# Eight experts in fixed order and two passes, with all weights kept on chip, after a linear attention

## The chip, the cores and the metric

One core of a Trainium2 chip runs the whole program in one launch. The metric is the device time of one execution in microseconds (us); the median of a few runs counts.

A core has five engines with one instruction queue each, worked in order: TensorE (PE; its weight loads are listed apart as PEld), VectorE (DVE), ScalarE (ACT), GpSimd (POOL) and SyncE (SP). Sixteen DMA engines move data. Loads and stores issued by SP form the hardware queue (q1 in the profile), those issued by POOL the software queue (q0).

## The reference

The input has 4 batches of 8 heads with 768 positions of 64 elements. The first half is a linear attention with decay: per head, `out[i] = sum over j <= i of lam^(i-j) (q_i . k_j) v_j`, worked in blocks with a running 64x64 state. Its result, read as 3072 tokens of 512 elements, is `x`. The second half is a mixture of 8 experts with balanced routing:

```python
logits = x @ w_gate                       # 3072 x 8
order = np.argsort(-logits.flatten())     # all token-expert pairs, best first
for idx in order:
    tok, e = idx // 8, idx % 8
    if assigned[tok] >= 0 or counts[e] >= 384: continue
    assigned[tok] = e; counts[e] += 1
for e in range(8):
    h = np.maximum(x[assigned == e] @ w1[e], 0)   # 512 -> 1024
    out[assigned == e] = h @ w2[e]                # 1024 -> 512
```

Each expert gets exactly 384 tokens. The greedy order can be run in steps: up to the moment when a first expert is full, every token simply goes to its best expert (the filling step); then the tokens that are left choose among the others until the next is full, and so on. On the inputs used here the filling step ends with 356, 363, 375, 340, 384, 317, 327 and 350 tokens at the eight experts, and 260 tokens are left.

## The kernel before

**Attention** (`_Attn.run`, L903). 24 tiles of 128 tokens. An iteration loads q, k and v of tile s+3 by SP (L747 to L751), turns and multiplies, writes the finished tile s-1 to `x_dram` by SP (L876) and prepares k and v of tile s+2 (`prep`, L754). The buffers of the loads hold four tiles, and SP works its queue in order, so a load stands behind the write of an earlier tile. The eight logits of each token are left in the tile `logits` (L901).

**Routing** (`_Router`). `phase1` runs once all logits are there: the range of the values (L102 to L124), three rounds that narrow down the rank at which the first expert is full (`count`, L148: a comparison on DVE, 24 matmuls, a sum, a maximum), the slots, and the list `perm` of the first full expert's tokens (L227 to L230). A second set of 24 matmuls (L272) gathers the tokens that are left and the token table `tok1`. `phase(i)` then finds the next full expert, again in three rounds (L327 to L343), and its `perm`.

**Experts** (`_Moe`). Which expert comes next is known only from the routing, so its number is read into a register by POOL (L469), and POOL issues its two weight loads of 1 MB each as stored on chip (L475, L477; float32 in memory, cast to bf16 on the way; three buffers each), three gathers of 128 token rows (L461), and, as the expert's results come, three scatters of 128 rows to the output (L503). `ffn` (L480) turns the rows (L486), multiplies by `w1` (L492, 32 matmuls of 384 columns), and by `w2` (L499, 24 of 512 columns). A scatter waits until the scatter before it has landed, since both write the same tensor at rows unknown beforehand.

`_check_and_mend` (L526) runs a slow exact path if a flag says that the fast routing does not hold.

What sets the order: a scheduler places the instructions of each engine's queue by their dependences and its own estimate of time; the order of the Python lines is only its starting point. For the expert stretch of the new kernel PE, POOL and DVE are taken out of that and follow the order of the code.

Of the kernel before, what the change touches and what calls it, by code (L numbers as in the profile page):

```python
# [13 lines left out]
I32 = mybir.dt.int32  # L14
AX = mybir.AxisListType
# [7 lines left out]
class _Router:  # L23


    def __init__(self, ctx, tc, identf, identb):
        nc = tc.nc
        self.nc, self.tc = nc, tc
        self.identf, self.identb = identf, identb
        P = 128  # L30
        self.rc = ctx.enter_context(tc.tile_pool(name="rconst", bufs=1))

    def constants(self):
        nc, rc, P = self.nc, self.rc, 128
        i_kt = rc.tile([P, P, 24], BF16, name="i_kt")
        nc.gpsimd.iota(i_kt, pattern=[[1, P], [0, 24]], base=0, channel_multiplier=0,
                       allow_small_or_imprecise_dtypes=True)
        self.i_kt = i_kt
        i_j = rc.tile([P, 29, 24], BF16, name="i_j")
        nc.gpsimd.iota(i_j[:, 0:5], pattern=[[1, 5], [0, 24]], base=24, channel_multiplier=0,  # L40
                       allow_small_or_imprecise_dtypes=True)
        nc.gpsimd.iota(i_j[:, 5:29], pattern=[[1, 24], [0, 24]], base=0, channel_multiplier=0,
                       allow_small_or_imprecise_dtypes=True)
        self.i_j = i_j
        i_t = rc.tile([P, 29, 24], BF16, name="i_t")
        nc.gpsimd.iota(i_t, pattern=[[0, 29], [128, 24]], base=0, channel_multiplier=0,
                       allow_small_or_imprecise_dtypes=True)
        self.i_t = i_t
        i_p = rc.tile([P, 1], F32, name="i_p")
        nc.gpsimd.iota(i_p, pattern=[[0, 1]], base=0, channel_multiplier=1,  # L50
                       allow_small_or_imprecise_dtypes=True)
        self.i_p = i_p
        i_e = rc.tile([P, 8], F32, name="i_e")
        nc.gpsimd.iota(i_e, pattern=[[1, 8]], base=0, channel_multiplier=0,
                       allow_small_or_imprecise_dtypes=True)
        self.i_e = i_e
        kio = []
        for r, sc in enumerate((65536, 256, 1)):
            i_k = rc.tile([P, P], BF16, name=f"i_k{sc}")
            nc.vector.tensor_scalar(i_k, i_kt[:, :, 0], float(sc), None, OP.mult)  # L60
            kio.append(i_k)
        self.kio = kio
# [928 lines left out]
```

## Time and profile before

| | |
|---|---|
| runs | 393.26 us median of 3 (392.68 to 394.55) |
| profiled execution | 392.43 us, its span 390.7 us |
| attention, to the last logits | 0 to 163.4 us |
| routing to the first row list | 163.4 to 188.5 us |
| first turn of the first expert | 199.2 us |
| last matmul of the last expert | about 371 us |
| last scatter issued | 384.4 us |
| PE busy | 262.1 us (67%), mean granted clock 0.847 |
| DMA | 52.00 MB written, q0 36.5% and q1 30.0% of 16 engines |

How to read it: the span runs from the first to the last instruction of the profiled execution. A busy share is a mean over stages with different limits: in the attention DVE, PE and ACT are all near 75% busy, and in the expert stretch PE stands still for ten microseconds at a time while the DMA engines are full. The granted clock is the share of full speed at which TensorE ran; it takes two levels, 2.4 GHz (1.0) and 1.2 GHz (0.5).

### The profile page before, as it was taken

How to read it: one execution, taken by the hardware profiler on the slowest of the kernel's cores; microseconds unless marked ns; L12 is line 12 of the kernel's file. 1: busy time of each engine (PE TensorE's matmuls, PEld its weight loads, DVE VectorE, ACT ScalarE, POOL GpSimd, SP SyncE). 2: the span in 40 equal slices, each digit the busy share in tenths (PEclk: the TensorE clock that was granted, in tenths of full speed). 3: DMA queues.
4: the chain of work that ended last, by engine and by line, in shares of the span. 5: the costliest groups of instructions: out<-in, count | busy, mean ns of one | idle time of the engine just before them, and what ended most of it. 6: DMA issues, size and time to landing. Idle time of an engine off the chain costs nothing. (4 is left out here: it accounts for less than half of the span.)

```text
span 390.7 us, 8518 instructions
## 1 busy us (share of the span) xinstructions
PE 262.1 (67%) x3323; PEld 179.6 (46%) x3331; DVE 196.1 (50%) x701; ACT 170.2 (44%) x308; POOL 160.9 (41%) x180
## 2 busy tenths in 40 slices
PE   2787787878787778542679459850774939796900
PEld 2567666766666676342334234520433525443400
DVE  3977677676866777668347630700523516400000
ACT  4686776767675766300024124520332414443400
POOL 5857565566566655201301415152351422514122
PEclk9999999999999999755559758995695886997975
DMA  8988878687776821100940997549396793999321
GB/s 154 217 188 173 194 161 181 154 181 172 156 177 149 202 63 37 56 0 4 180 74 6 190 222 95 109 95 196 100 167 142 137 174 79 156 209 142 93 81 55
DMA packets 96973, 52.00 MB, mean 133 GB/s; under 512 B 76960, under 2 KB 88224, under 8 KB 96928
## 3 DMA queue, kind: packets, MB, share of 16 engines
q0 software_dynamic: 17920, 26.22, 36.5%
q1 hardware_dynamic: 79008, 25.19, 30.0%
q8 instruction: 27, 0.44, 0.5%
q14 instruction: 18, 0.15, 0.1%
HBM read 58.74 MB, written 12.58 MB: 183 GB/s over the span
## 5 line engine op out<-in xcount | busy, mean ns | idle before, releaser
L492 PE MATMUL p<-xeT,w1t 128*128 128x384 bf16 x256 | 60.2, 382 | 4.9 <-ACT xeT L487 4.9
L503 POOL DMA_INDIRECT out_dram<-oe,perm x24 | 24.2, 1008 | 88.7 <-ACT hT L495 30.3
L812 POOL TENSOR_SCALAR_AFFINE_SELECT sp<-sp 128x512 f32<-128x512 f32 x48 | 34.9, 735 | 41.4 <-DVE sp L809 41.4
L487 ACT COPY xeT<-pt 128x512 bf16<-128x512 bf16 x24 | 14.1, 586 | 82.3 <-PE pt L486 68.0
L495 ACT ACTIVATE hT<-p 128x384 bf16<-128x384 f32 x64 | 31.4, 491 | 33.7 <-PE p L492 29.0
L499 PE MATMUL p<-w2t,hT 128*128 128x512 bf16 x184 | 42.9, 379 | 1.3 <-DMA w2t<-in_moe_w_dram 0.9
L809 DVE TENSOR_TENSOR sp<-S,sp 128x512 bf16<-128x512 f32 x48 | 33.0, 736 | 21.4 <-ACT sp L808 20.4
L486 PE MATMUL pt<-identb,xe 128*128 128x128 bf16 x96 | 12.9, 271 | 41.9 <-DMA xe<-x_dram,perm 35.0
L808 ACT CAST sp<-S 128x512 bf16<-128x512 f32 x48 | 32.1, 740 | 16.9 <-PE S L803 16.9
L492 PEld LDWEIGHTS <-w1t 128*128 128x128 bf16 x256 | 26.7, 112 | 22.5 <-issue 15.5
L766 POOL TENSOR_TENSOR vl<-vs,vh 128x512 bf16<-128x512 f32 x24 | 27.8, 1160 | 16.4 <-ACT vh L764 16.0
L461 POOL DMA_INDIRECT xe<-x_dram,perm x24 | 24.6, 1024 | 23.6 <-PE p L492 9.3
L761 POOL TENSOR_TENSOR vs<-vf,lamneg 128x512 f32<-128x512 f32 x24 | 27.8, 1159 | 3.8 <-ACT lamneg L731 3.8
L803 PE MATMUL S<-qh,kT 64*128 64x128 f16 x384 | 28.7, 221 | 0.9 <-DVE sp L809 0.5
L486 PEld LDWEIGHTS <-xe 128*128 128x128 bf16 x96 | 8.5, 117 | 45.0 <-DMA xe<-x_dram,perm 37.7
L499 PEld LDWEIGHTS <-hT 128*128 128x128 bf16 x192 | 18.5, 97 | 22.1 <-issue 1.1
L502 ACT COPY oe<-p 128x512 f32<-128x512 f32 x24 | 14.1, 586 | 33.1 <-PE p L499 26.4
L843 PE MATMUL XL<-vh,sp 128*128 128x64 bf16 x384 | 23.2, 194 | 7.3 <-POOL sp L812 6.9
L775 PE MATMUL kT_ps<-identf,kp 128*128 128x128 f32 x96 | 16.1, 291 | 14.1 <-DVE kp L759 14.1
L843 PEld LDWEIGHTS <-sp 128*128 128x128 bf16 x576 | 20.2, 98 | 11.0 <-POOL sp L812 10.4
L475 POOL DMA_DIRECT2D w1t<-in_moe_w_dram x8 | 6.7, 836 | 44.3 <-DVE Z L407 24.1
L764 ACT CAST vh<-vs 128x512 bf16<-128x512 f32 x24 | 14.9, 621 | 19.0 <-POOL vs L761 19.0
(244 smaller groups left out, 630.4 us busy)
## 6 DMA issues: line engine op xcount, KB each, us to landing
w1t<-in_moe_w_dram POOLq DMA_DIRECT2D x8, 1024.0 KB
w2t<-in_moe_w_dram POOLq DMA_DIRECT2D x8, 1024.0 KB, 12.0
qf<-in_q_dram SPq DMA_DIRECT2D x24, 256.0 KB, 3.5
kf<-in_k_dram SPq DMA_DIRECT2D x24, 256.0 KB, 4.3
vf<-in_v_dram SPq DMA_DIRECT2D x24, 256.0 KB, 5.0
x_dram<-xs SPq DMA_DIRECT2D x24, 256.0 KB, 2.2
xe<-x_dram,perm POOLq DMA_INDIRECT x24, 9.5
out_dram<-oe,perm POOLq DMA_INDIRECT x24, 9.1
```

The source lines that it names most:

```text
L461: nc.gpsimd.indirect_dma_start(out=xe[:, c, :], out_offset=None, in_=self.x_dram, in_offset=bass.IndirectOffsetOnAxis(ap=perm[:, c : c + 1 ...
L492: nc.tensor.matmul(p1, w1t[:, kc, fc * P : (fc + 1) * P], xeT[:, kc].rearrange("p c s -> p (c s)"), start=(kc == 0), stop=(kc == 3))
L495: nc.scalar.activation(hT[:, fc, :], p1, ACT.Relu)
L499: nc.tensor.matmul(p2, hT[:, kc, c * P : (c + 1) * P], w2t[:, kc, :], start=(kc == 0), stop=(kc == 7))
L503: nc.gpsimd.indirect_dma_start(out=self.out, out_offset=bass.IndirectOffsetOnAxis(ap=perm[:, c : c + 1], axis=0), in_=oe, in_offset=None, ...
L761: nc.gpsimd.tensor_tensor(vs, vf, self.lamneg[:, t, :, None].to_broadcast([P, 8, 64]), OP.mult)
L766: nc.gpsimd.tensor_tensor(vl, vs, vh, OP.subtract)
L803: nc.tensor.matmul(S[a][:, hp, :], kT[r, hp, :, ks], qq[r, hp, :], start=(i == 0), stop=(i == 2))
L808: nc.scalar.copy(s[:, :, :, 1], S[a])
L809: nc.vector.tensor_tensor(s[:, :, :, 0], S[a], s[:, :, :, 1], OP.subtract)
L812: nc.gpsimd.affine_select(out=sf, in_=sf, compare_op=OP.is_ge, fill=0.0, base=0, pattern=[[0, 4], [1, P]], channel_multiplier=-1)
L843: nc.tensor.matmul(X[a][:, hp, :], sp[a][:, hp, :, ss], vv[:, h, :], start=(first and hp == 0 and i == 0), stop=(i == 2), skip_group_check ...
```

## The change

Three things are rewritten together.

Routing: the range of the values is taken from the first 18 tiles while the attention still runs, and the rank of each tile's tokens is prepared beside it (`ranges`, `ranks`, called by the hook). The three counting rounds use 128, 64 and 64 thresholds, the last two with half-size comparisons. After the filling step each expert's first 256 tokens are known. The remaining six steps (`steps`) run piece by piece between the experts' matmuls; the code waits in between by an estimate (`WAIT`).

Experts: they come in the order 0 to 7. Pass one takes 256 rows of each (two row blocks), pass two the last 128. All sixteen weight tiles have their own place on chip. Nine loads are written in the attention's code (`load_w(0)` to `load_w(8)`), seven between the experts.

Where the moves land is read from the instruction order. First POOL in the early attention. `vs` and `vl` prepare v of a tile, `sp` is its masked score tile, `w_0_78` and `w_0_79` are w1 and w2 of expert 0. Before:

```order
L812 AFFINE_SELECT sp_225<-sp_225 128x512
L766 TENSOR_TENSOR vl<-vs,vh 128x512
L812 AFFINE_SELECT sp_229<-sp_229 128x512
L761 TENSOR_TENSOR vs<-vf,lamneg 128x512
L766 TENSOR_TENSOR vl<-vs,vh 128x512
L812 AFFINE_SELECT sp_333<-sp_333 128x512
```

And POOL at the same place now:

```order
L979 AFFINE_SELECT sp_238<-sp_238 128x512
L979 AFFINE_SELECT sp_242<-sp_242 128x512
L73 AFFINE_SELECT slt<-slt 128x128
L533 DMA w_0_78<-in_moe_w_dram 128x4x1024
L928 TENSOR_TENSOR vs<-vf,lamneg 128x512
L535 DMA w_0_79<-in_moe_w_dram 128x8x512
L933 TENSOR_TENSOR vl<-vs,vh 128x512
L979 AFFINE_SELECT sp_346<-sp_346 128x512
```

The scheduler has moved the first loads from the end of the attention, where the code writes them, to its second tile; all nine stand between the selects of tile 0 and those of tile 7.

Second, POOL when pass one begins. `perm` lists rows, `xe` are gathered rows, `oe` a finished block; DMASW is a slot of the software queue, of which there are eight. Before, at the first experts:

```order
L461 DMA xe<-x_dram,perm 128x512 [waits DMASW1_49]
L503 DMA out_dram<-oe,perm 3072x512 [waits DMASW2_49,Activation_49]
L469 TENSOR_LOAD ei [waits DVE_49]
L469 ISA x2
L475 ISA
L475 DMA w1t<-in_moe_w_dram 128x4x1024 [waits DMASW3_49]
```

And now:

```order
L550 DMA xe<-x_dram,perm_4180 128x512 [waits DMASW0_49]
L550 DMA xe<-x_dram,perm_4180 128x512 [waits DMASW1_49]
L533 DMA w_5_3839<-in_moe_w_dram 128x4x1024 [waits DMAHW3_49,DMAHW2_49,DMASW2_49]
L535 DMA w_5_3840<-in_moe_w_dram 128x8x512 [waits DMASW3_49]
L600 DMA out_dram<-oe,perm_4055 3072x512 [waits DMASW4_49,Activation_49]
L600 DMA out_dram<-oe,perm_4055 3072x512 [waits DMASW5_49,DMASW4_49,Activation_49]
L550 DMA xe<-x_dram,perm_4180 128x512 [waits DMASW6_49,PE_49]
L550 DMA xe<-x_dram,perm_4180 128x512 [waits DMASW7_49]
L533 DMA w_6_3841<-in_moe_w_dram 128x4x1024 [waits DMASW0_49]
L535 DMA w_6_3842<-in_moe_w_dram 128x8x512 [waits DMASW1_49]
L600 DMA out_dram<-oe,perm_4055 3072x512 [waits DMASW5_49,DMASW2_49,Activation_49]
```

Loads no longer wait for a register, but the pairs of experts 5, 6 and 7 each stand right ahead of the first scatter of experts 0, 1 and 2; the second scatter waits for the slot of the first.

Third, PE where the first expert starts. L486 and L564 are the first turns. Before, they come right behind the matmuls of the left-over tokens:

```order
L272 LDWEIGHTS A
L272 MATMUL psC<-R,A 128x207
L486 LDWEIGHTS xe
L486 MATMUL pt<-identb,xe 128x128
L486 LDWEIGHTS xe
```

Now two counting rounds and the token table (`psT`, 24 matmuls, L339) come in between; the last rows ahead of the turns are:

```order
L388 LDWEIGHTS ind
L388 MATMUL cps<-oh,ind 128x8
L404 LDWEIGHTS ones_572
L404 MATMUL nps<-S,ones_572 128x8
L564 LDWEIGHTS xe
L564 MATMUL pt<-identb,xe 128x128
```

So the first expert's turns stand behind the second round of the first later step. The diff, cut to its core:

```diff
+    def ranks(self, L, a, b):
...
+        V.tensor_tensor(self.ind1[:, :, a:b], q1[:, None, :].to_broadcast([P, P, n]),
+                        self.i_kt[:, :, a:b], OP.is_ge)
...
+            for hh in range(2):
...
+                V.tensor_tensor(ind[:, 0:64, ts], zq[:, None, ts].to_broadcast([P, 64, 12]),
+                                self.i_kt[:, 0:64, ts], OP.is_ge)
...
+        yield perm0.rearrange("p (e j) -> p e j", j=3)
...
+        psC = ps.tile([P, 18, 5], F32, tag="pos")
...
+            psT = ps.tile([P, 2, 24], F32, tag="pos")
...
+    def steps(self, rest):
...
+        for i in range(1, 7):
...
+            for r in range(3):
+                ind = sp.tile([P, 5, P], BF16, tag="indc")
+                for c in range(5):
+                    V.tensor_scalar(ind[:, c, :], self.kvec[r], zr[:, c : c + 1], None, OP.is_le)
...
+                yield self.WAIT[0 if r else (1 if i > 1 else 2)]
...
+                yield self.WAIT[3]
...
+                if i == 1 and r == 0:
+                    yield rest()
...
+    def load_w(self, m):
+        e = m // 2
+        if m % 2 == 0:
+            self.nc.gpsimd.dma_start(out=self.w1t[e], in_=self.w1r[e])
+        else:
+            self.nc.gpsimd.dma_start(out=self.w2t[e], in_=self.w2r[e])
...
+    def gather(self, perms):
+        nc, P = self.nc, 128
+        xe = self.mp.tile([P, 2, 512], BF16, tag="xe", bufs=4)
...
+                for kc in range(4):
+                    nc.tensor.matmul(p1[:, f, 0:n, :], self.w1t[e][:, kc, fc * P : (fc + 1) * P],
+                                     j["xeT"][:, kc, 0:n, :], start=(kc == 0), stop=(kc == 3),
+                                     skip_group_check=True)
...
+        oe = self.mp.tile([P, 512], F32, tag="oe", bufs=4)
+        nc.scalar.copy(oe, p2)
+        nc.gpsimd.indirect_dma_start(
+            out=self.out, out_offset=bass.IndirectOffsetOnAxis(ap=j["perms"][c], axis=0),
+            in_=oe, in_offset=None, bounds_check=3071, oob_is_err=False)
...
+    with tc.manual_schedule(engines={E.PE, E.Pool, E.DVE}):
...
+            for n in range(16):
+                if n == 0:
+                    yield ("land", 6.0)
+                    yield from moe.turn(jobs[0])
+                if n == 8:
+                    yield ("routed", None)
+                    yield from moe.turn(jobs[8])
+                yield from moe.up(jobs[n], n % 8)
+                if n < 15 and n != 7:
+                    yield from moe.turn(jobs[n + 1])
+                if jobs[min(n + 3, 15)] is None:
+                    ahead(n + 3)
+                for _ in range(2):
+                    if later:
+                        moe.load_w(later.pop(0))
+                for c in range(len(jobs[n]["perms"])):
+                    yield from moe.down(jobs[n], n % 8, c)
...
+        def hook(s):
+            if s == 2:
+                router.constants()
+            if 19 <= s <= 21:
+                router.ranges(logits, 18, attn.pt, "T", s - 19)
+            if s == 22:
+                router.ranks(logits, 0, 10)
+            if s == 23:
+                router.ranks(logits, 10, 20)
+            if s == 24:
+                router.ranks(logits, 20, 23)
+            if 21 <= s <= 24:
+                moe.load_w(s - 21)
...
+    for m in range(4, 9):
+        moe.load_w(m)
+    fi = _route_and_moe(ctx, tc, logits, router, moe, range(9, 16))
```

## Rows read from the trace of the kernel before

**Rows 1.** Waits, summed: who, for whom, us, times, longest
```profile
ACT xeT L487 <- PE pt L486: 68.0, 22, 34.8
```
**Rows 2.** Tile `xe`: from issue to landing
```profile
DMA to landing us min/median/max: 8.8/9.5/11.2
```
**Rows 3.** Timeline of POOL: start, us, what, [idle before]
```profile
238.40 0.97 POOL L477 DMA_DIRECT2D w2t<-in_moe_w_dram  x1
239.67 1.05 POOL L503 DMA_INDIRECT out_dram<-oe,perm  x1 [0.30 <-issue]
250.14 1.00 POOL L503 DMA_INDIRECT out_dram<-oe,perm  x1 [9.41 <-ACT hT L495]
```
**Rows 4.** Timeline of POOL, the last scatter
```profile
384.45 0.98 POOL L503 DMA_INDIRECT out_dram<-oe,perm  x1 [2.51 <-issue]
```
**Rows 5.** Windows: length, busy of PE, PEld, DVE, ACT, POOL, clock, DMA share, GB/s
```profile
60.00:80.00 20.00, 15.88 (x336) 13.68 (x337) 15.50 (x26) 14.47 (x26) 11.85 (x13) 1.00 0.77 171
203.00:371.00 168.00, 117.95 (x732) 63.39 (x740) 55.32 (x406) 57.13 (x109) 53.56 (x55) 0.81 0.74 135
```
**Rows 6.** Windows with one DMA queue full: attention's loads, then weights
```profile
8.00:10.00 2.00, 1.76 (x8) 1.43 (x8) 0.66 (x3) 1.99 (x5) 0.93 (x1) 1.00 1.34 218
187.00:188.00 1.00, 1.00 (x17) 1.00 (x17) 0.23 (x1) 0.00 (x0) 0.00 (x0) 0.50 1.10 209
```
**Rows 7.** The page's DMA issues, and timelines of SP and ACT
```profile
kf<-in_k_dram SPq DMA_DIRECT2D x24, 256.0 KB, 4.3
...
64.56 0.65 SPq L749 DMA_DIRECT2D kf<-in_k_dram  x1
...
71.74 0.78 ACT L758 CAST kp<-kf 128x512 f16<-128x512 f32 x1
...
77.79 0.79 ACT L758 CAST kp<-kf 128x512 f16<-128x512 f32 x1
```
**Rows 8.** Timeline of DVE, routing: last logits, counting rounds two and three, row list
```profile
163.27 0.17 DVE L901 COPY logits<-Lo 128x8 f32<-128x8 f32 x1 [0.52 <-PE Lo L899]
...
172.29 1.83 DVE L153 TENSOR_TENSOR ind<-z,i_kt 128x1536 bf16<-128x1536 bf16 x2
...
176.10 1.83 DVE L153 TENSOR_TENSOR ind<-z,i_kt 128x1536 bf16<-128x1536 bf16 x2
...
188.33 0.17 DVE L230 TENSOR_REDUCE perm<-pe 128x3 int32<-128x6 f32 x1 [1.10 <-PE pe L227]
```
**Rows 9.** Timeline, routing matmuls, the first turn and the first finished block
```profile
186.54 1.75 PE L227 MATMUL pe<-B1v,A 128*128 128x6 bf16 x24 [4.41 <-DVE B1v L222]
...
194.48 4.93 PE L272 MATMUL psC<-R,A 128*128 128x207 bf16 x13
...
199.22 0.60 PE L486 MATMUL pt<-identb,xe 128*128 128x128 bf16 x4
...
212.97 0.59 ACT L502 COPY oe<-p 128x512 f32<-128x512 f32 x1 [1.53 <-PE p L499]
```
**Rows 10.** Timeline of DVE, one counting round of a later step to the next
```profile
206.77 0.91 DVE L331 TENSOR_SCALAR ind<-i_k,zn 128x128 bf16<-128x128 bf16 x5
...
208.84 0.91 DVE L331 TENSOR_SCALAR ind<-i_k,zn 128x128 bf16<-128x128 bf16 x5
```
**Rows 11.** Timeline of PE, matmuls back to back
```profile
203.06 1.44 PE L492 MATMUL p<-xeT,w1t 128*128 128x384 bf16 x4 [0.67 <-ACT xeT L487]
...
206.09 0.97 PE L492 MATMUL p<-xeT,w1t 128*128 128x384 bf16 x5
...
207.12 0.32 PE L492 MATMUL p<-xeT,w1t 128*128 128x384 bf16 x1
...
215.24 1.89 PE L499 MATMUL p<-w2t,hT 128*128 128x512 bf16 x8
```
**Rows 12.** The page's DMA queues: packets, MB, share of 16 engines
```profile
q0 software_dynamic: 17920, 26.22, 36.5%
q1 hardware_dynamic: 79008, 25.19, 30.0%
```

More of the change, by code (lines that the diff above doesn't have):

```diff
@@ L167, in phase1 @@
+        cps = ps.tile([P, 8], F32, tag="cnt")
+        for t in range(23):
+            nc.tensor.matmul(cps, self.ind1[:, :, t], ohb[:, t, :], start=(t == 0), stop=False)
+        self.ranks(L, 23, 24)
+        nc.tensor.matmul(cps, self.ind23, ohb[:, 23, :], start=False, stop=True)
+        _, nm1 = settle(cps, self.ones[64])
+        self.more(23, 24)
         z2 = sp.tile([P, 24], BF16, name="z2")
-        nc.vector.tensor_scalar(z2, z12, nm1, 200.0, OP.subtract, OP.min)
+        V.tensor_scalar(z2, self.q2, nm1, 100.0, OP.subtract, OP.min)
@@ new lines, in down @@
+    def down(self, j, e, c):
+        nc, P = self.nc, 128
+        p2 = self.mps.tile([P, 512], F32, tag="p2")
+        for kc in range(8):
+            nc.tensor.matmul(p2, j["hT"][:, kc // 2, kc % 2, c, :], self.w2t[e][:, kc, :],
+                             start=(kc == 0), stop=(kc == 7))
+            if kc % 2 and kc < 7:
+                yield 0.43
+        oe = self.mp.tile([P, 512], F32, tag="oe", bufs=4)
[3 more added lines that the diff above has]
+            in_=oe, in_offset=None, bounds_check=3071, oob_is_err=False)
+        yield 0.43
@@ new lines, in ffn, with _route_and_moe, ahead, experts @@
+    def ffn(self, e, perms):
+        j = self.gather(perms)
+        for g in [self.turn(j), self.up(j, e)] + [self.down(j, e, c) for c in range(len(perms))]:
+            for _ in g:
+                pass
+def _route_and_moe(ctx, tc, L, router, moe, later):
+    E = mybir.EngineType
+    with tc.manual_schedule(engines={E.PE, E.Pool, E.DVE}):
+        gen = router.phase1(ctx, L)
+        jobs = [None] * 16
+        perm0 = next(gen)
+        for e in range(2):
+            jobs[e] = moe.gather([perm0[:, e, 0:1], perm0[:, e, 1:2]])
+        later = list(later)
+        perm1 = perm2 = None
+        def ahead(n):
+            if perm1 is None or n > 15:
+                return
+            if n < 8:
+                jobs[n] = moe.gather([perm1[:, n, 0:1], perm1[:, n, 1:2]])
+            elif perm2 is not None:
+                jobs[n] = moe.gather([perm2[:, n - 8 : n - 7]])
+        def experts():
+            for n in range(16):
[15 more added lines that the diff above has]
+                    yield from moe.down(jobs[n], n % 8, c)
+        ex = experts()
+        t, done, want = 0.0, False, None
+        r_at = None
+        def route():
+            nonlocal r_at, perm1, perm2, t
+            while True:
+                got = next(gen, None)
+                if got is None:
+                    r_at = None
+                    return
+                if isinstance(got, float):
+                    r_at = t + got
+                    return
+                if perm1 is None:
+                    perm1 = got
+                    ahead(2)
+                    moe.load_w(later.pop(0))
+                else:
+                    perm2 = got
+                    for n in (8, 9, 10):
+                        ahead(n)
+        route()
+        while not done or r_at is not None:
+            if r_at is not None and (r_at <= t or done or
+                                     (want is not None and (want[0] == "routed" or r_at <= want[1]))):
+                t = max(t, r_at) + 0.2
+                route()
+                continue
+            if want is not None:
+                t = t + 5.0 if want[0] == "routed" else max(t, want[1])
+                want = None
+            got = next(ex, None)
+            if got is None:
+                done = True
+            elif isinstance(got, tuple):
+                want = got
+            else:
+                t += got
```

776 lines of the change are left out of this document (396 added, 380 removed).

## The prediction

> **What bounds the kernel now.** I read the slices of the span first, then the windows, the summed waits, and POOL's timeline. The program has three stretches. In the attention (to 163.4 us) the engines share the work: DVE, PE and ACT are each near 75% busy, and the DMA engines move 171 GB/s [rows 5]. Routing is a chain on DVE and PE. The expert stretch, 203 to 371 us, is bound by no engine: PE is busy for 118 of 168 us, POOL and DVE for a third [rows 5]. What ends last there is a gather: turning the rows waits 68 us in sum [rows 1], because a gather lands 9.5 us after its issue [rows 2], behind the two weight loads that the same step has just put into the same queue. The last scatters then stand alone, one per 3.5 us, since each waits for the landing of the one before (2.51 idle + 0.98 busy), and 6.2 us pass from the start of the last to the end of the span, so 2.7 us beyond its own 3.5 [rows 4].
>
> **Attention with nine weight loads in it.** The change takes the loads off the expert stretch; it pays for that here. A weight tile is 1.05 MB as stored, and the software queue alone writes 209 GB/s, so one load fills the DMA engines for 5.1 us, nine for 45.6. A tile of the attention moves four times 0.262 MB; its loads alone saturate at 218 GB/s [rows 6], which makes 4.8 us, while the tile takes 6.06 us of compute (77.79 - 71.74) [rows 7]. The nine loads stand in POOL's queue between the selects of tile 0 and tile 7, about 6.5 tiles apart. In that stretch the DMA engines have 45.6 + 6.5 x 4.8 = 76.8 us of work against 6.5 x 6.06 = 39.4 us of compute: 37 us too much. Loads run ahead: the k issued at 64.56 lands some 4.3 us after it and is read at 77.79, three ACT reads later by the order of the code, so 8 us are in hand [rows 7]. That leaves 29 us by which the attention ends later; afterwards compute at 6.06 us a tile sets the pace again and nothing is caught up. No trace of before shows both queues full at once, so this has ends: 0, if the two queues use different limits of an engine and the loads hide altogether (a gain is excluded: traffic is only added), and 45.6, if none of it hides. I take 29, the sum from the saturated rows. POOL's own issue of the nine, 0.97 each [rows 3], stands beside a POOL that is 59% busy here [rows 5]; without that cover it would be 9 us.
>
> DVE gets the ranges and ranks, some 60 small instructions (about 12 us) in the last six tiles, where it has 4.5 us free in 20 [rows 5], 8 us in six tiles, and more once no tile is prepared any more. I take +2; ends 0 and 12.
>
> **From the last logits to the first expert.** Before, 163.44 to 188.5 us [rows 8]. Five microseconds of range finding go to the attention; what is left of them for the last tile is about six DVE operations, 1.2 us. Rounds two and three, 3.81 us each (176.10 - 172.29), lose half of their 1.83 us of comparison and keep the rest: 2.9. The row list for experts 0 and 1 is ready at about 163.4 + 1.2 + 1.5 + 2 x 2.9 + 8.2 = 180 us, 8 earlier, and its gathers find the queue empty. But PE's order does not let the first turns follow. In between stand: 2 us of DVE for the left-over table; 24 matmuls of 90 columns (between 0.073 us at 6 columns and 0.38 at 207 [rows 9], so 0.2 each, 4.8); 2.2 us to the first thresholds; a round, 1.6; the token table on DVE, 1.6; 24 matmuls of 48 columns, 3.4; ten small DVE operations and the second round, 3.6. That sums to 19 us and ends at 199, where the first turn stood before (199.22) [rows 9]. So the shorter routing is given away to what was put ahead of the first turn; the weights being there gains nothing yet.
>
> **The expert stretch.** PE's work: at full clock a row of five matmuls of 384 columns takes 0.97 and a single one 0.32, so 0.16 each, and eight of 512 in 1.89 are 0.22 each [rows 11]. Pass one has 256 up matmuls of 256 columns (0.107: 27), pass two 256 of 128 (0.055: 14), both together 192 down matmuls (42), turns and routing pieces about 15 (estimate from the same spacings). That is 98 us, from 199 to 297 if nothing stops it, plus a few us at the lower clock at the start.
>
> The scatters are a longer chain. There are still 24, each waits for the one before. The first is ready about 12 us after the first turn (before: 212.97 - 199.22 = 13.75 with three row blocks instead of two [rows 9]): at 211. Alone a scatter costs 3.5 us [rows 4]; behind a weight load it costs 10.5 (239.67 to 250.14, with a load issued just ahead) [rows 3]. By POOL's new order the pairs of experts 5, 6 and 7 each stand straight ahead of a scatter, that of experts 0, 1 and 2. So 21 x 3.5 + 3 x 10.5 = 105 us. Two gathers of 1.3 us fit nearly into the 2.5 us between scatters; the three issued at once after the last routing step and the weight issues do not: +4. End: 211 + 105 + 4 + 2.7 = 322.7. PE runs beside it and is held back where four finished blocks wait, so its 98 us do not count again.
>
> The routing beside it: a round takes 2.07 us [rows 10], a step with its tail about 8, six steps and the end 55 us, from 190 to some 250; pass two begins near 280. It is hidden; if each step stopped PE for its whole excess over the code's estimate, about 1.2 us, it would be 7 us on a PE that has 20 to spare.
>
> **Sum.** 322.7 + 29 + 2 = 353.7 us of span; 1.7 us lie around the span (392.43 - 390.7), so 355.4 for an execution like the profiled one, whose time is 0.8 below the median of the runs: 356 us.
>
> **Rivals.** *The loads hide in the attention.* For it: the share of the DMA engines reads 1.34 when the loads saturate but only 0.77 in the steady attention [rows 5, 6], so much of their time may be free for another queue. Against: in bytes, 171 of 218 GB/s are in use. With 0 to 10 us instead of 29: about 332.
>
> *The loads of q, k and v starve.* If the two queues take turns packet by packet, the weights' packets are the long ones: 36.5% of 390.7 us on 16 engines over 17920 packets is 127 ns, 30.0% over 79008 is 24 ns [rows 12]. Then the attention's loads get 24/151 = 16% of the time while weights flow; the nine take 45.6/0.84 = 54 us, in which loads for 1.8 tiles come, with the 8 us in hand worth 19 us of compute: 35 us late, up to 45.6 if the prefetch cannot refill between pairs. About 368. No run of before shows it, since nothing but the weights' own queue is active when they load. The Trainium skill, DMA: Bandwidth & Descriptors, section Queues, rings and completion order, says that each DMA engine goes round its queue rows packet by packet, and that is the rule which speaks against putting large loads beside many small ones; no row here shows it.
>
> *TensorE stays at its lower clock: slower than before.* Over the expert stretch the granted clock was 0.81 [rows 5], the rest of full speed lost after the waits for gathers; at the lower level four up matmuls take 1.44 us instead of five in 0.97 [rows 11]. If the many small routing matmuls and stops of pass one hold the clock at 0.5, the 98 us of PE become 196: 199 + 31 + 196 + 7 for the last scatter = 433. It decides from the point where PE's end passes the scatters' gain: at full clock PE's path ends at 335, before ends at 391, so from 56 us more, a little over half of the stretch at the lower level. Against: in 203 to 217 us before, with counting rounds between expert matmuls, the spacing fell to that of the full clock at 206 [rows 11].
>
> *The change does not do what it says.* If an expert had fewer than 256 tokens at the filling step, the slow exact path would run after the fast one. The inputs give 317 to 384, so it is left out but for 1%.
>
> **Chances.** Forecast 0.50 (own range 343 to 364), hidden 0.24 (325 to 343), starved 0.17 (364 to 378), lower clock 0.07, the rest 0.02. A measurement here can tell about 0.5% (2 us) from no change. Faster 0.92, same 0.01, slower 0.07. The range leaves out the lower clock and the outer end of the hidden case, and so runs from 327 to 386.
>
> **What would show it.** In the profile after: nine weight loads issued before some 90 us and tiles of more than 6.1 us there, DMA share near its maximum; the last logits near 194 instead of 163.4; the row list 17 us after them, the first turn 36 us after them; three scatters of 10 us early in pass one, then a beat of 3.5 us to the end; PE's clock at 1.0 for most of the stretch. I am wrong in the attention if its tiles keep 6.1 us (hidden) or if q, k and v land 20 us after issue (starved); wrong in the expert stretch if POOL is not waiting for its own scatters when PE stands still.

## The result, and the profile after

| | before | after |
|---|---|---|
| median of the runs | 393.08 us (392.68 to 394.55) | 374.79 us (374.2 to 375.93) |
| ratio | | 0.9532, interval 0.9498 to 0.9566 |
| span of the profiled execution | 390.7 us | 373.2 us |
| last logits | 163.4 us | 197.8 us |
| first turn of the first expert | 199.2 us | 230.6 us |
| first scatter, last scatter | | 242.5 us, 365.3 us |
| PE busy | 262.1 us (67%) | 268.0 us (72%) |

The kernel became 18.3 us faster. I had forecast 356 us, 37 us less than before. The direction and the order of events came as predicted; the expert stretch was 17 us longer and the attention 3 us longer than the sum. Executions of one kernel differ by up to 3.5%, so the times below are medians, while places in time come from one profiled execution each.

The attention first. Here are the windows of the kernel after, with the columns of [rows 5]:

```profile
40.00:60.00 20.00, 6.46 (x110) 5.44 (x108) 4.39 (x9) 4.19 (x8) 5.07 (x6) 0.67 1.18 219
...
80.00:100.00 20.00, 13.35 (x183) 11.41 (x184) 9.40 (x16) 10.15 (x18) 7.61 (x9) 0.61 1.08 218
```

From 40 to 60 us the engines do 30 to 41% of their work of before, PE 6.46 of 20 us where before it had 15.88 [rows 5], while the DMA engines move 219 GB/s, as much as when one queue alone saturates them [rows 6]. Who waits stands in the summed waits of the kernel after (us, times, longest):

```profile
ACT kp L925 <- DMA kf<-in_k_dram: 27.6, 7, 11.1
...
ACT oe L599 <- DMA out_dram<-oe,perm: 22.8, 4, 10.8
```

Before, ACT waited for k once, for 3.0 us; now it loses 27.6 us in seven waits. DVE's timeline shows the end of the attention and the row list, against 163.27 and 188.33 in [rows 8]:

```profile
197.60 0.22 DVE L1068 COPY logits<-Lo 128x8 f32<-128x8 f32 x1
...
214.46 0.17 DVE L289 TENSOR_REDUCE perm<-pe 128x6 int32<-128x12 f32 x1 [1.11 <-PE pe L286]
```

PE's timeline of the kernel after shows what stands between the row list and the first turn (before: [rows 9]):

```profile
216.37 4.11 PE L303 MATMUL psC<-R,ind 128*128 128x90 f16 x24 [1.95 <-DVE R L300]
...
225.15 2.36 PE L339 MATMUL psT<-R,ind 128*128 128x48 f16 x24 [1.73 <-DVE R L336]
...
230.61 1.01 PE L564 MATMUL pt<-identb,xe 128*128 128x128 bf16 x8
```

Then POOL's timeline, with scatters (L600), gathers (L550) and weight loads (L533, L535); it answers to [rows 3, 4]:

```profile
242.53 1.07 POOL L600 DMA_INDIRECT out_dram<-oe,perm  x1 [6.60 <-ACT oe L599]
252.99 1.03 POOL L600 DMA_INDIRECT out_dram<-oe,perm  x1 [9.40 <-ACT oe L599]
...
256.72 0.83 POOL L533 DMA_DIRECT2D w<-in_moe_w_dram  x1
257.52 0.98 POOL L535 DMA_DIRECT2D w<-in_moe_w_dram  x1
258.80 1.06 POOL L600 DMA_INDIRECT out_dram<-oe,perm  x1 [0.30 <-issue]
273.26 1.03 POOL L600 DMA_INDIRECT out_dram<-oe,perm  x1 [13.40 <-ACT oe L599]
...
277.77 0.98 POOL L535 DMA_DIRECT2D w<-in_moe_w_dram  x1
279.06 1.06 POOL L600 DMA_INDIRECT out_dram<-oe,perm  x1 [0.30 <-issue]
294.30 1.03 POOL L600 DMA_INDIRECT out_dram<-oe,perm  x1 [14.19 <-ACT oe L599]
...
365.31 0.98 POOL L600 DMA_INDIRECT out_dram<-oe,perm  x1 [3.75 <-ACTq L696]
```

The three scatters behind the weight pairs hold the next one back for 10.46, 14.46 and 15.24 us. (The pair of the first was issued from 234.18 us on, 8 us ahead of its scatter; the other two stand right ahead of theirs, behind two gathers.) The releaser named is ACT's copy into a block buffer, but that copy itself waits for a landed scatter (the second row of the waits above), so both names point at the same landing. From 268 to 308 us PE does 24 us of work in 40, as these windows of the kernel after show:

```profile
268.00:288.00 20.00, 14.33 (x110) 9.70 (x109) 8.04 (x49) 4.37 (x7) 5.94 (x6) 0.83 0.77 138
288.00:308.00 20.00, 9.99 (x70) 6.46 (x67) 5.57 (x36) 5.56 (x10) 8.24 (x8) 0.74 0.51 107
```

### The profile page after: what moved, and what is told of

It reads as the page before. It is cut to its first block, busy times and chain, and to the rows that moved or that the text cites. A ratio compares the mean times of both kernels' runs of the same rounds, so it can differ in the third digit from the quotient of the medians.

```text
span 373.2 us, 8812 instructions
## 1 busy us (share of the span) xinstructions
PE 268.0 (72%) x3551; PEld 210.7 (56%) x3551; DVE 185.6 (50%) x587; ACT 168.2 (45%) x297; POOL 161.6 (43%) x189
## 5 line engine op out<-in xcount | busy, mean ns | idle before, releaser
L581 PE MATMUL p<-xeT,w 128*128 128x256 bf16 (+1 forms) x512 | 53.9, 262 | 17.7 <-ACT hT L586 16.4
L600 POOL DMA_INDIRECT out_dram<-oe,perm x24 | 24.3, 1014 | 81.0 <-ACT oe L599 49.6
L581 PEld LDWEIGHTS <-w 128*128 128x128 bf16 x512 | 42.0, 103 | 27.6 <-issue 19.3
L594 PE MATMUL p<-w,hT 128*128 128x512 bf16 x192 | 47.5, 392 | 0.0
L586 ACT ACTIVATE hT<-p 128x512 bf16<-128x512 f32 (+1 forms) x64 | 31.1, 491 | 22.4 <-PE p L581 16.6
L976 DVE TENSOR_TENSOR sp<-S,sp 128x512 bf16<-128x512 f32 x48 | 32.9, 734 | 15.4 <-ACT sp L975 15.2
L1010 PE MATMUL XL<-vh,sp 128*128 128x64 bf16 x384 | 27.7, 208 | 12.8 <-POOL sp L979 12.5
L550 POOL DMA_INDIRECT xe<-x_dram,perm x24 | 25.2, 1050 | 25.2 <-DVE B L294 11.2
L568 ACT COPY xeT<-pt 128x1024 bf16<-128x1024 bf16 (+1 forms) x16 | 12.8, 798 | 42.9 <-PE pt L564 42.7
L925 ACT CAST kp<-kf 128x512 f16<-128x512 f32 x24 | 18.9, 789 | 27.6 <-DMA kf<-in_k_dram 27.6
L926 DVE TENSOR_TENSOR kp<-kf,kp 128x512 f16<-128x512 f32 x24 | 19.6, 816 | 23.4 <-ACT kp L925 23.4
L942 PE MATMUL kT_ps<-identf,kp 128*128 128x128 f32 x96 | 19.3, 338 | 15.8 <-DVE kp L926 11.0
L970 PEld LDWEIGHTS <-kT 64*128 64x128 f16 x576 | 20.9, 104 | 10.3 <-issue 6.9
L1029 PE MATMUL stp<-vh,kp 128*128 128x128 bf16 x160 | 22.0, 252 | 4.7 <-ACT vh L931 3.9
```

Source lines behind the costliest of these rows:

```text
L550: nc.gpsimd.indirect_dma_start(out=xe[:, c, :], out_offset=None, in_=self.x_dram, in_offset=bass.IndirectOffsetOnAxis(ap=pm, axis=0), boun ...
L581: nc.tensor.matmul(p1[:, f, 0:n, :], self.w1t[e][:, kc, fc * P : (fc + 1) * P], j["xeT"][:, kc, 0:n, :], start=(kc == 0), stop=(kc == 3), ...
L586: nc.scalar.activation(hT[:, fp, :, 0:n, :], p1[:, :, 0:n, :], ACT.Relu)
L594: nc.tensor.matmul(p2, j["hT"][:, kc // 2, kc % 2, c, :], self.w2t[e][:, kc, :], start=(kc == 0), stop=(kc == 7))
L600: nc.gpsimd.indirect_dma_start(out=self.out, out_offset=bass.IndirectOffsetOnAxis(ap=j["perms"][c], axis=0), in_=oe, in_offset=None, bound ...
L970: nc.tensor.matmul(S[a][:, hp, :], kT[r, hp, :, ks], qq[r, hp, :], start=(i == 0), stop=(i == 2))
```

## The experiments

Two theories were to be tested. **A:** the attention's 34 us are DMA time of nine loads beside q, k and v. **B:** the chain of scatters, with the weight pairs in its queue, sets the length of the expert stretch. The rivals: the routing work beside the attention, TensorE's own pace, the later routing steps. Where a load is to start late, VectorE first writes one column of its tile from a logits tile, so that the scheduler cannot place the load earlier (`pin`).

**1. Nine loads at the attention's end.** The diff, with the pin:

```diff
+    def load_w(self, m, after=None):
...
+        if after is not None:
+            w = (self.w2t if m % 2 else self.w1t)[e]
+            self.nc.vector.tensor_copy(w[:, 0, 0:1], after)
...
-                moe.load_w(s - 21)
+                moe.load_w(s - 21, logits[:, s - 2, 0:1])
...
-        moe.load_w(m)
+        moe.load_w(m, logits[:, 23, 0:1])
```

> Nine weight loads tied to the last tiles of the attention (two fall in the last two tiles, seven behind the last select), nothing else changed. Theory A (attention): the 34 us by which the last logits came later are DMA time of the nine loads beside q, k and v. Then the last logits return to 164 to 167 us, the first turn follows 33 to 36 us later (200), and the span is 373 - 32 = 341 (338 to 346). Rival: the routing work that now runs beside the attention (ranges, ranks on VectorE) or the new order costs a good part of it; then the last logits stay at 175 or later and the span above 350.

Measured: 354.12 us (351.85 to 358.97), ratio 0.8981 [0.8944, 0.9017]. The profiled execution took 358.97 us. Its last logits came at 175.97, just in the rival's range: 21.6 us of the 34 are gone, 12.7 are not. In the expert stretch the long periods stayed, and the first turn waited 4.5 us for a gather that stood behind seven loads. So early loads are the larger part of the 34 us, and something else is in it: the logits of tile 19 come at 155.3, before at 145.7, and no load is issued until then (the first at 155.99).

**2. The other seven loads ahead of the experts.** Attention as in the changed kernel; loads 9 to 12 behind it, the first of them pinned to the last logits, 13 to 15 behind the first gathers:

```diff
+        while later:
+            moe.load_w(later.pop(0))
...
-    for m in range(4, 9):
-        moe.load_w(m)
+    for m in range(4, 13):
+        moe.load_w(m, logits[:, 23, 0:1] if m == 9 else None)
...
```

> Attention as in the changed kernel; the last seven loads are issued right behind the attention and behind the first gathers, none ahead of a scatter. Theory B (the chain of scatters paces the experts, and weight pairs ahead of a scatter cost 10 to 15 us each): the three long periods (10.5, 14.5, 15.2 us) become 4 us each, so the span falls by about 27 us, to 346 (340 to 352), and POOL still waits for its own scatters to the end. Rival (TensorE's work with the routing pieces paces them, the scatters only follow): at most 8 us are won, span 365 or more.

Measured: 340.72 us (340.36 to 345.0), 0.8664 [0.8639, 0.8689], at the lower end of the forecast. The first scatter starts where it did (241.98 against 242.53). POOL's timeline of this run, scatters L603, gathers L553:

```profile
241.98 1.05 POOL L603 DMA_INDIRECT out_dram<-oe,perm  x1 [8.43 <-ACT oe L602]
245.56 1.00 POOL L603 DMA_INDIRECT out_dram<-oe,perm  x1 [2.53 <-ACT hT L589]
246.87 1.04 POOL L553 DMA_INDIRECT xe<-x_dram,perm  x1 [0.30 <-PE p L584]
248.21 1.02 POOL L553 DMA_INDIRECT xe<-x_dram,perm  x1 [0.30 <-issue]
250.63 1.03 POOL L603 DMA_INDIRECT out_dram<-oe,perm  x1 [1.40 <-ACT oe L602]
254.21 1.00 POOL L603 DMA_INDIRECT out_dram<-oe,perm  x1 [2.54 <-ACT hT L589]
...
335.07 0.98 POOL L603 DMA_INDIRECT out_dram<-oe,perm  x1 [3.38 <-ACTq L700]
```

No period is long any more, and the 23 periods take 93.1 us (335.07 - 241.98) instead of 122.8 (365.31 - 242.53). The loads in the chain's way cost 29.7 us, B's price. The window of this run from the first turn to the last product shows what sets the pace without them, a PE that is busy nearly throughout:

```profile
230.84:333.20 102.36, 99.28 (x924) 69.91 (x936) 41.18 (x246) 55.86 (x104) 41.74 (x42) 0.97 0.45 103
```

**3. Loads spread over the attention, the rest ahead of the experts.** One load each at tiles 0, 4, 8, 12 and 16, four at the last tiles, the seven as in 2:

```diff
+            if s in (2, 6, 10, 14, 18):
+                moe.load_w((s - 2) // 4, logits[:, s - 2, 0:1])
             if 21 <= s <= 24:
-                moe.load_w(s - 21)
+                moe.load_w(s - 16, logits[:, s - 2, 0:1])
```

> Five loads at tiles 0, 4, 8, 12 and 16, four at the last tiles, four behind the last logits, three behind the first gathers. Theories A and B together: each early load (5.1 us) uses up the 1.26 us that four tiles of the attention have free each, so the last logits come at 164 to 169; the first turn 33 us later; then no scatter behind a load, 23 periods of 3.6 to 4.0 us and 8 us of tail: 199 + 12 + 87 + 8 = 306, and TensorE's 98 us (from 199) end at 297 to 310 beside it. Span 306 to 322. If the two gains share a cause, or queues taking turns packet by packet make even a single load late for its tile, 325 to 345.

Measured: 320.09 us (318.16 to 321.07), ratio 0.8152 [0.8119, 0.8185], as forecast and far below both kernels. The windows of this run, first in the attention, then in the expert stretch:

```profile
60.00:90.00 30.00, 25.18 (x522) 22.44 (x520) 22.55 (x44) 21.01 (x38) 19.08 (x22) 0.94 1.07 226
...
225.00:245.00 20.00, 19.87 (x186) 14.38 (x187) 13.40 (x79) 10.81 (x17) 9.01 (x9) 1.00 0.40 96
245.00:265.00 20.00, 19.84 (x180) 13.92 (x182) 14.39 (x89) 11.13 (x18) 8.13 (x8) 1.00 0.27 79
```

The DMA engines are as full as in the changed kernel (226 GB/s), but the engines keep their work. The logits of tile 19 in DVE's timeline of this run and of the kernel before:

```profile
146.03 0.14 DVE L1072 COPY logits<-XL 128x8 f32<-128x8 f32 x1
...
145.70 0.17 DVE L901 COPY logits<-XL 128x8 f32<-128x8 f32 x1 [0.53 <-PE XL L899]
```

Up to there the attention with five loads keeps the time of before. The last logits, with four more loads beside the last tiles, come at 168.4, 5.1 us later than before. In the expert stretch PE now has no gap, 19.8 of 20 us.

**4. No chain of scatters, loads where the change has them.**

```diff
-            out=self.out, out_offset=...
+            out=self.outs[self.n % 4], out_offset=...
```

> The scatters go in turn to four tensors, so that none waits for the landing of the one before; three quarters of the output are thus left out. Loads stay where the changed kernel has them. Theory B: without the chain the long periods behind weight pairs hold back only the blocks that wait in four buffers; TensorE's 98 us from 231 at about the clock of the changed kernel set the end: span 340 to 352. Rival (TensorE and the routing pieces set the pace already): 366 to 373.

Measured: 343.41 us (339.02 to 349.49), 0.8687 [0.8609, 0.8765]. The first and the last scatter in POOL's timeline:

```profile
239.92 1.06 POOL L600 DMA_INDIRECT out_dram<-oe,perm  x1 [6.34 <-ACT oe L599]
...
333.14 0.98 POOL L600 DMA_INDIRECT out<-oe,perm  x1 [2.78 <-ACT oe L599]
```

That is 93.2 us, the same as in run 2. Taking away the loads or taking away the chain gives the same 30 us: neither costs them alone. A scatter has to wait for the landing of one that lies behind two loads in the queue, and only both together make that long.

**5. No load beside the attention.** Loads 0 to 3 behind the last logits, 4 to 8 behind the first gathers:

```diff
-            if 21 <= s <= 24:
-                moe.load_w(s - 21)
...
+        for _ in range(4):
+            m = later.pop(0)
+            moe.load_w(m, None if m else L[:, 23, 0:1])
...
+        for _ in range(5):
+            moe.load_w(later.pop(0))
...
```

> No weight load at all beside the attention: four behind the last logits, five behind the first gathers, the rest as in the changed kernel. Theory A: the last logits at 164 to 168 us, that is 30 us or more of the 34 were the loads. Rival, from the run with late loads (176): the new order of the attention with ranges and ranks beside it costs about 12 us by itself, with a granted clock below 1.0 there; then 174 to 178. The span follows: 341 (336 to 348) or 352 (348 to 358).

Measured: 367.27 us (362.4 to 368.4). DVE's timeline has the logits of tile 17, the first instruction of `ranges`, the last logits and the row list at

```profile
139.92 0.15 DVE L1076 COPY logits<-XL 128x8 f32<-128x8 f32 x1
...
140.61 0.29 DVE L106 TENSOR_REDUCE v<-logits 128x18 f32<-128x144 f32 x1
...
170.11 0.22 DVE L1076 COPY logits<-Lo 128x8 f32<-128x8 f32 x1
...
187.18 0.17 DVE L289 TENSOR_REDUCE perm<-pe 128x6 int32<-128x12 f32 x1 [1.10 <-PE pe L286]
```

The last logits lie between the forecasts: without any load the attention ends 6.8 us later than before (163.27 [rows 8]). Against this run the nine loads cost 197.6 - 170.1 = 27.5 us, but that is a rough price. Runs 2, 4, 7 and 8 issue the same nine loads early, and their last logits come at 196.7, 195.2, 191.3 and 196.6, so it is 21 to 27.5. And the scheduler has not left the attention's instructions as they were: in the changed kernel and in run 3 VectorE works `kp` right ahead of a tile's logits (145.41 and 146.03 in run 3), here behind them (120.98 and 120.89). Run 3 with its five loads has the logits of tile 19 at 146.0, this run without a load at 152.0. If the changed kernel's order costs nothing by itself, the loads are all of the 34 us.

The span met neither forecast: the first scatter came at 223.7, but the second 18.4 us later, behind the loads that I had put behind the gathers. That is B once more.

**6. The routing work moved back behind the attention**, on run 5:

```diff
-            if 19 <= s <= 21:
-                router.ranges(logits, 18, attn.pt, "T", s - 19)
+            if s == 25:
+                for part in range(3):
+                    router.ranges(logits, 24, attn.pt, "T", part)
...
```

> The run without loads in the attention, with the range of the values taken from all 24 tiles and the ranks of the tokens prepared behind the last logits (as before the change) instead of beside the last tiles. The last logits came at 170.1 there, 163.3 before the change. If the routing work beside the attention costs those 7 us: last logits at 163 to 165, and about 8 us more from there to the first turn. If it is the new order of the attention's instructions: 168 to 171 still, and the span longer by what the routing takes, 371 to 376.

Measured: 373.96 us (370.73 to 377.61). The last logits came at

```profile
172.04 0.17 DVE L1076 COPY logits<-Lo 128x8 f32<-128x8 f32 x1 [0.53 <-PE Lo L1074]
...
197.34 0.17 DVE L289 TENSOR_REDUCE perm<-pe 128x6 int32<-128x12 f32 x1 [1.10 <-PE pe L286]
```

no earlier than in run 5, so the routing work is not what costs the 6.8 us. The rows of run 5 say the same: its tile 17 is 5.7 us late already (139.92, before 134.18), ahead of the first instruction of `ranges`. Its first tile is 3.2 us late (29.99 against 26.80), the next twenty 4.2 us together. What does it is not shown. Two candidates are left: the order of the attention's instructions, and the granted clock, which from 20 to 140 us was 1.00 before, 0.95 in run 5, 0.96 here and 0.93 in run 1. The clock alone does not explain it, since the run spread_d below has 0.96 there and tile 19 at 145.5. Neither was tried alone. The row list follows the last logits after 25.3 us here and after 17.1 in run 5: work taken ahead is worth 8.2 us.

**7. The first turn ahead of the token table**, in the changed kernel:

```diff
-                    yield ("land", 6.0)
+                    yield ("land", 0.5)
```

> In the changed kernel only the wait that the code assumes before the first expert is cut from 6.0 to 0.5, so that PE's queue has the first turn ahead of the token table and the second round. Theory C (what stands ahead of the first turn holds it back, and the scatter chain behind it carries that to the end): the first turn moves from 230.6 to 222 to 224, the first scatter from 242.5 to 235, the span falls by 6 to 8 us to 366. Rival (the later routing steps or the weight pairs set the end): the steps start later by the first expert's matmuls and the span stays at 371 to 376.

Measured: 374.32 us (373.27 to 375.72), 0.9529 [0.9475, 0.9582]: no difference. The turn did move, to 22.7 us behind the last logits instead of 33.0 (which came 6.3 us earlier in this profile than in that of the changed kernel, at 191.3). POOL's timeline of this run:

```profile
229.96 0.82 POOL L533 DMA_DIRECT2D w<-in_moe_w_dram  x1
230.75 0.96 POOL L535 DMA_DIRECT2D w<-in_moe_w_dram  x1
232.01 1.06 POOL L600 DMA_INDIRECT out_dram<-oe,perm  x1 [0.30 <-ACT oe L599]
250.04 1.03 POOL L600 DMA_INDIRECT out_dram<-oe,perm  x1 [16.97 <-ACT oe L599]
```

With both together the first scatter is issued 10.5 us earlier, the second only 3: it waits behind the same loads. The gathers of pass two were issued 5.3 us later (324.60 against 319.27), and the last scatter 0.2 us earlier. The rival holds.

**8. One load per expert instead of a pair.**

```diff
-                for _ in range(2):
+                for _ in range(1):
                     if later:
                         moe.load_w(later.pop(0))
```

> The changed kernel, but each of experts 0 to 5 issues one weight load ahead of its scatters instead of experts 0 to 2 two each. Theory B by the queue (a scatter lands only when the loads issued before it have drained, 5.1 us each, whatever stands behind what): six periods of about 9 us instead of 10.5, 14.5 and 15.2, the same sum, span 370 to 378. If a load costs more than its drain (a price per pair of gathers and loads, or per switch between loads and scatters), six disturbed periods cost more than three: 380 or more. If single loads hide beside a scatter's own wait of 2.5 us: 355 to 365.

Measured: 375.09 us (370.0 to 377.44), the changed kernel's time. POOL's timeline:

```profile
266.78 0.83 POOL L533 DMA_DIRECT2D w<-in_moe_w_dram  x1
267.91 1.03 POOL L600 DMA_INDIRECT out_dram<-oe,perm  x1 [0.30 <-issue]
276.55 0.99 POOL L600 DMA_INDIRECT out_dram<-oe,perm  x1 [7.61 <-ACT oe L599]
```

The six scatters behind one load hold the next back for 6.6 to 11.2 us, 9.0 on average, as forecast, and first to last scatter take 125.5 us (after: 122.8). One by one or in pairs, the loads cost the chain the same.

**9. What binds when the loads are out of the way.** Run 3 without the chain (the edit of 4), and run 3 with half of the first product left out:

```diff
-                for kc in range(4):
+                for kc in (0, 3):
```

> The spread loads with the scatters going in turn to four tensors (three quarters of the output left out): what is left is TensorE's own pace. If the chain of scatters still sets the end once the loads are out of its way: first turn at 205, TensorE's 98 us and a scatter's tail, span 303 to 309. If TensorE with the routing pieces has become the limit: within 3 us of the 316 with the chain.

> The spread loads with half of the first product's matmuls left out (the hidden layer is incomplete): TensorE has about 20 us less to do, the scatters and loads are the same. If the chain sets the end: first scatter 2 us earlier, then periods of 3.5 us where they were late for TensorE; span 306 to 312. If TensorE is the limit: 20 us less, 298 or below. If the routing steps are: 314 to 316.

Measured: 319.86 us (318.88 to 320.78) and 319.54 us (316.81 to 320.91), both the 320.1 of run 3. Without the chain PE goes on at its own pace, busy for 100.5 of the 104.2 us from the first turn to the last product; with less on PE (85.0 of 96.2 us) the chain does, as POOL's timeline of the second shows:

```profile
239.61 1.00 POOL L603 DMA_INDIRECT out_dram<-oe,perm  x1 [2.88 <-ACT hT L589]
240.92 1.04 POOL L553 DMA_INDIRECT xe<-x_dram,perm  x1 [0.30 <-issue]
242.27 1.02 POOL L553 DMA_INDIRECT xe<-x_dram,perm  x1 [0.30 <-issue]
243.59 1.03 POOL L603 DMA_INDIRECT out_dram<-oe,perm  x1 [0.30 <-issue]
...
276.69 0.99 POOL L603 DMA_INDIRECT out_dram<-oe,perm  x1 [2.51 <-ACT hT L589]
280.23 0.98 POOL L603 DMA_INDIRECT out_dram<-oe,perm  x1 [2.55 <-ACT hT L589]
```

The scatters take 91.0 us here (218.59 to 309.59) and 92.6 in run 3, where PE is busy for 99.3 of 102.2 us. From the first turn to the end of the span pass 111.5 us in run 3, 112.9 without the chain and 109.0 with less on PE; but there the first turn came 3.8 us later (208.7 against 204.9), which takes the 2.5 us back. So both are limits, and neither edit alone wins more. No run makes both edits at once, so a third limit close below them, such as the routing steps, is not excluded. The rows also give the chain's beat here: 3.5 us alone, 4.0 us where two gathers are issued.

**10. Other placements of run 3.** Pins two tiles older, so that a pair of loads was issued at 137 and 140 us, while q, k and v still came, and no pins on the loads behind the last logits (spread_b, and spread_early with the edit of 7); only two loads at the end and five behind the first gathers (spread_c); run 3 with one pin left on the loads behind the last logits (spread_d):

```diff
-                moe.load_w(s - 16, logits[:, s - 2, 0:1])
+                moe.load_w(s - 16, logits[:, s - 4, 0:1])     # spread_b, spread_early
...
+            if s in (22, 24):                                  # spread_c
+                moe.load_w(s // 2 - 6, logits[:, s - 2, 0:1])
...
-        moe.load_w(m, logits[:, 23, 0:1])
+        moe.load_w(m, logits[:, 23, 0:1] if m == 9 else None)  # spread_d
```

> As the spread loads, but without what stopped queues at the attention's end: the loads of the last tiles wait for logits two tiles older, the loads into freed space wait for nothing on VectorE. The last logits come at 164 to 168 instead of 168.5 and the ranking of the last tile follows at once (171.8 before): span 310 to 313 instead of 316. Rival (the tail is bound by VectorE's ranks): 315 to 318.

> The run before with the first turn ahead of the token table as well. Theory B and C: the first turn 25 us behind the last logits instead of 33, 23 periods of about 4 us behind it: span 302 to 306. Rival (with the chain started earlier, pass two waits for the last routing step, whose list came at 264 us, 15 us before it was used): half of that or nothing, 307 to 313.

> The spread loads with only two loads at the attention's end instead of four, four behind the last logits and five behind the first gathers. The attention's end has less beside it: last logits at 164 to 166 instead of 168.5, ranking at once; the loads behind the gathers fill the queue until 220 and push the first scatters by up to 4 us. Span 310 to 316. If the loads at the attention's end are not what delays it, or the gathers of the third expert stand behind five loads and hold TensorE: 317 to 324.

> The spread loads, of which three of the four behind the last logits no longer wait for a write by VectorE. There the ranking of the last tile stood 2.7 us behind that write, which waited for the last rows of x to be written. Last logits unchanged (168.5), ranking 2.5 us earlier, and with the same expert stretch the time falls from 320.1 to 317 to 318. If the first expert waits for its gather or weights anyway: 319 to 321.

Measured: 327.32, 329.87, 326.16 and 318.4 us (315.01 to 325.98). The first three missed. In spread_b DVE's timeline has two neighbouring tiles at

```profile
139.50 0.14 DVE L1074 COPY logits<-XL 128x8 f32<-128x8 f32 x1
155.31 0.17 DVE L1074 COPY logits<-XL 128x8 f32<-128x8 f32 x1 [0.55 <-PE XL L1072]
```

15.8 us apart instead of 6, and 16.1 in spread_early: the 9.8 us too many are about the drain of a pair beside the tiles. In spread_early the turn came 3.5 us earlier but pass two's gathers 10.3 us later than in spread_b (284.19 against 273.86), and nothing was won. In spread_c the second scatter came 13 us behind the first, as in run 5. spread_d cannot be told from run 3.

## Why the prediction was right in direction and wrong in size

The forecast span was 353.7 us, the measured one 373.2. The 19.5 us between them by the prediction's own steps:

| step | forecast | measured | error |
|---|---|---|---|
| last logits (163.4 + 31) | 194.4 | 197.8 | +3.4 |
| from there to the first turn | 35.6 | 32.8 | -2.8 |
| first turn to first scatter | 12 | 11.9 | -0.1 |
| three periods behind weight pairs | 31.5 | 40.2 | +8.7 |
| the other twenty | 70 + 4 | 82.6 | +8.6 |
| from the start of the last scatter | 6.2 | 7.9 | +1.7 |

**The step that failed is the sum of the expert stretch, "21 x 3.5 + 3 x 10.5 = 105".** That the chain of scatters would decide, and that the pairs would stand in its way, was right (runs 2 and 4). Both prices were too low. The 10.5 us of [rows 3] came from a scatter with one load straight ahead of it, and I used them for a pair. Where a pair and two gathers stand there, 14.5 and 15.2 us pass; that the first period took the 10.5 of the forecast is luck, since its pair had 8 us to drain ahead. In sum the loads cost 29.7 us (run 2) where I had 3 x 7 = 21 beyond the beat. And the beat of 3.5 us was read at the very end of the program, where no gather is issued [rows 4]; with two gathers it is 4.0 (run 9). I had reckoned that gathers fit nearly into the 2.5 us of a scatter's wait, and gave them and the weight issues 4 us in all. The twenty periods lie 12.6 us above 20 x 3.5. Of these, 4.6 are in the two periods of 5.8 us in which POOL issues two gathers and a weight pair one after the other (252.99 to 258.80 above, and 273.26 to 279.06), and 1.8 in the one with three gathers (317.99 to 323.24). The other 6.2 us are spread over periods of 3.8 to 4.8 us, whose causes were not separated. TensorE's own sum was right: 98 us forecast, 99.3 busy (run 2).

**The attention: the size nearly right, its make-up not shown.** 31 us were forecast and 34.4 measured, 28 in the profile of run 7. The sum over saturated DMA engines said 29 for the loads; the runs leave them 21 to 34, depending on what the attention costs without them (run 5), so the nearness is in part luck. The 2 us for the routing work beside it are shown by no run; moved behind the attention it brought the last logits no earlier, and it pays back 8.2 us there (run 6). Two smaller slips: 1.05 MB at 209 GB/s are 5.0 us a load, not 5.1; and "nothing is caught up" is not so, since tile 7 is 37 us late (107.4, before 70.3) and the last 34.

**The slack per tile was right and I did not use it.** 4.8 us of loads in 6.06 us of compute leave 1.26 us a tile, a load per four tiles; so spaced, five loads left the logits of tile 19 where they were (run 3).

**Routing: nearly right.** The row list came 17 us behind the last logits (214.46 - 197.8 = 16.7), the first turn 33 us behind them, 36 forecast; "the shorter routing given away to what was put ahead of the first turn" is true as a place, but taking that away gains nothing while the loads stand behind it (run 7). The later steps are hidden: the last row list was there at 310.8 us, the first turn of pass two at 322.7, right behind the last product of pass one.

**The rivals.** Hidden loads: refuted, the attention ends 34 us later, but true of spaced ones. Starved q, k and v: its sign came in part, and its price cannot be told from mine. Single landings of k took up to 21.1 us (median 5.2), where I had named 20. Counted from the packets in the trace, the weights' queue moved 3.06 MB from 40 to 60 us and the queue of q, k, v and x 1.28 MB, against 3.48 MB before; the latter had 27% of the DMA time, where the rival said 16%. The rule of the Trainium skill, DMA: Bandwidth & Descriptors, section Queues, rings and completion order, that an engine goes round its queue rows packet by packet, agrees in kind: the queue with the long packets got the larger part. The rival's 35 us for the attention and my 31 both lie near the 34 measured, and the measured time lies in the rival's range of 364 to 378; but the 17 us that my sum lacked are in the expert stretch, of which the rival says nothing. Spaced loads starve q, k and v no less while they move (39 of 178 GB/s from 32 to 36 us in run 3), yet the small loads catch up in between (244 GB/s from 68 to 76 us), so the tiles lose nothing. Lower clock: where PE stood still most, the granted clock was 0.74 (288 to 308 us), and from the first turn to the last product 0.88; with the stops gone it is 1.00 (225 to 265 us in run 3). PE never became the slower limit.

Open: what costs run 5's attention 6.8 us, with it the exact price of the nine loads, and the 1.7 us at the end.

## What to carry to other kernels

Price a chain of dependent transfers at a place that looks like the new one: with the same loads and gathers in the same queue, not where the queue is empty. Before large loads are moved beside small ones, divide the load's drain by the free DMA time of a step, and leave that many steps between two loads; here a burst of nine cost 21 to 34 of its 45 us, and five at that spacing nothing. When two limits are nearly equal, as PE and the scatters were here, an edit of either shows next to nothing; look in each run at which of the two waits.

## What the runs showed of the hardware

With both queues busy, the DMA engines moved 190 to 219 GB/s over windows of 20 us in the changed kernel, 226 in run 3 and at most 240 in any run (spread_b, 60 to 80 us); one queue alone moved 209 and 218 [rows 6]. Two queues do not add up: they share about one limit, and while both had work the weights' queue took 73% of the DMA time (40 to 60 us, after). The share read 1.18 at 219 GB/s and 1.07 at 226, so the bytes tell the limit better than the share.

A scatter right behind weight loads in POOL's queue holds the next one back until these have drained: 3.5 to 4 us with none, 7 to 11 with one (run 8), 14 to 15 with two.

In the changed kernel writes issued by SP for `x_dram` occupied its queue for 8.5 and 9.0 us each at 46 and 69 us, beside the weight loads, against 0.34 later in the attention (a load of k or v up to 6.6 against 0.5 to 1.8), so that the next loads of q, k and v were also issued late.
